# Feed-forward products of a two-layer transformer kernel as pairs of 64-row tiles

## The chip, the cores and the metric

One core of a Trainium2 chip. The metric is device time in microseconds (us). Five engines run side by side, each through its own queue in order: TensorE (PE; its weight loads are listed apart as PEld), VectorE (DVE), ScalarE (ACT), GpSimd (POOL) and SyncE (SP), which issues the DMAs. PE accumulates into PSUM, eight banks of 128 partitions by 512 float32; the other operands lie in SBUF, 128 partitions wide.

## The reference

Two identical layers over 2048 tokens of width 448: multi-query attention (16 heads of 28, one shared key and value head), then a SwiGLU feed-forward with 1792 hidden columns. Each half normalises its input and adds its result to the residual.

```python
def _B_ref(x, w_gate, w_up, w_down):
    g = _silu(x @ w_gate)
    u = x @ w_up
    return (g * u) @ w_down

x = A_x
x = x + _A_ref(_layernorm(x, axis=-1), A_wq, A_wk, A_wv, A_wo)
x = x + _B_ref(_layernorm(x, axis=-1), B_w_gate, B_w_up, B_w_down)
x = x + _A_ref(_layernorm(x, axis=-1), A_wq, A_wk, A_wv, A_wo)
x = x + _B_ref(_layernorm(x, axis=-1), B_w_gate, B_w_up, B_w_down)
```

## The kernel before

All products but those of values and transposes use a shortened float32 (`F32R`). To keep the precision, each operand is split into a high and a low part, and a product is the sum of high by high, high by low and low by high.

The feed-forward is cut into **units**: one unit is one slice of 128 hidden columns (`fc`, 14 of them) for one block of 512 tokens (`c`, 4 of them). The slices run in groups of two (`groups`), and within a group the order is block by block, for each block both slices (`n` = 0, 1): 8 units a group, 7 groups, 56 units a layer, 112 in all. The width of 448 is four chunks: three of 128 rows and one of 64. The last chunk is stacked: the token tile `xh[:, 3]` holds the high part in rows 0 to 63 and the low part in rows 64 to 127, and the weights' chunk is loaded twice, one copy below the other.

`unit` (L683) does this. On PE, `product_T` (L258) gives gate's product into one PSUM bank with 11 matmuls of 128 rows (three for each of the three full chunks, two for the stacked one), then up's product into a second bank with 11 more. ACT takes the silu of gate's bank (L695), DVE multiplies it by up's bank (L696), ACT rounds the result to the high part of h (L697), and DVE takes the low part (L698). `flush` (L679) then issues what an earlier unit left in `pend`: its `down` (L635), 12 matmuls, for each of four token tiles three into one of the four banks `HIGH`; and behind a block's second slice `accumulate` (L643), four adds of these banks to the residual `xres` on DVE (L647). So the down products of a unit stand on PE behind the products of the next one. The banks `LOW` serve gate and up by turns, two units deep.

The token tiles come from `turned` (L673): 16 transposes on PE (`flip`, L242), copies of the high part on ACT, low parts on DVE, and then `norm` (L236) of the block after, whose statistics, scaling and shifting run on DVE with a step on POOL between. In the first group this stands in the second unit (n = 1) of blocks 1 and 2, ahead of `flush`; `rest` (L716) calls it once more ahead of the first of its units, for block 1. The first two units of a layer (block 0) are issued inside the attention, ahead of `rest`.

In the last group of layer 0, `accumulate` also issues the statistics and scaling of the next layer's first normalisation, and two blocks are turned and projected to queries at once. `weights` (L156) loads and splits a slice of weights (DMA, then POOL) three slices ahead. `stack` (L306) brings the queries of one of 16 steps of the attention from DRAM into one of three tiles `qts`.

All engines run in the order in which the code issues the work (`manual_schedule`, L82); what waits for what is found from the tiles that are read and written.

Of the kernel before, what the change touches and what calls it, by code (L numbers as in the profile page):

```python
# [8 lines left out]
F32 = mybir.dt.float32  # L9
# [6 lines left out]
P = 128  # L16
S = 2048
D = 448
# [44 lines left out]
def forward(  # L63
# [67 lines left out]
    def dma(dst, src):  # L131
        nc.sync.dma_start(dst.bitcast(F32), src.bitcast(F32))  # L132
# [69 lines left out]
            part(z, load(z))  # L202
        return [], (wh, wl)

    def xtile(pool):
        return (
            pool.tile([P, 4, 512], F32R, name="xh"),
            pool.tile([P, 3, 512], F32R, name="xl"),
        )

    def norm_steps(c, pool=pers):
# [29 lines left out]

    def flip(got, tiles, ks=range(4), place=None):  # L242

        xh, xl = tiles
        for k in ks:
            pt = place if place is not None else bank(LOW)[1]
            for t in range(4):
                nc.tensor.transpose(pt[:, P * t : P * t + P], got["x"][:, t, P * k : P * k + P], ident)  # L248
            if place is not None:
                nc.vector.tensor_copy(xh[:, k, :], pt)  # L250
            else:
                nc.scalar.copy(xh[:, k, :], pt)
            if k < 3:
                nc.vector.tensor_tensor(xl[:, k, :], pt, xh[:, k, :], ALU.subtract)
            else:
                nc.vector.tensor_tensor(xh[64:128, k, :], pt[64:128, :], xh[64:128, k, :], ALU.subtract)

    def product_T(po, a_h, a_l, tiles, tick=None):  # L258

        xh, xl = tiles  # L260
        seq = []
        for k in range(3):
            seq += [(a_h[k], xh[:, k, :]), (a_h[k], xl[:, k, :]), (a_l[k], xh[:, k, :])]
        seq += [(a_h[3], xh[:, 3, :]), (a_l[3], xh[:, 3, :])]
        for i, (a, b) in enumerate(seq):
            nc.tensor.matmul(po, a, b, start=(i == 0), stop=(i == len(seq) - 1))  # L266
            if tick:
                tick()

    GR = [(c, g) for c in range(NC) for g in range(NG)]  # L270

    class Attention:
# [129 lines left out]
        def project(self):  # L402

            c, m = self.order[self.seen]
            for f in self.plan.get((self.seen, 0), ()):
                f()
            for o in self.order[self.seen : self.seen + 2]:
                if o[1] == 3:
                    self.turned(o[0])
            load = self.waiting.pop(0) if self.waiting else None  # L410
            self.q(c, m)
            if load:
                load()
            for f in self.plan.get((self.seen, 1), ()):
                f()
            self.seen += 1
            if c == 0 and m < 3:
                if not full and m < 2:
# [63 lines left out]
        def scores(self, ff):  # L482
            next(switch)
            with tc.tile_pool(name=f"at{self.layer}", bufs=1) as wp:
# [104 lines left out]
                ff.norms[1] = got1  # L589
                for i in range(len(GR)):  # L590
                    for k2 in range(NT // 2):
                        if k2 == 2 and 2 < i + 2 < len(GR):
                            self.stack(i + 2)
                        if k2 == 5 and i + 2 < len(GR) and not full:
                            self.high(i + 2)
                        if i in (2, 3) and k2 == 4:
                            load_wo(i - 2)
                        if k2 == 4 and 10 < i <= 11 + FG:
                            ff.W[i - 11] = weights(i - 11)

                        free = cycle(i, k2)
                        if k2 == 5 and i + 1 < len(GR) and full:
                            self.places[i + 1](free[:, 0, :])
                        if i == 6 and 0 < k2 < 5:
                            flip(got, X0, [k2 - 1], free[:, 0, :])
                        while late:
                            pv(*late.pop(0))
                        late += [(i, 2 * k2), (i, 2 * k2 + 1)]
                        if 8 * i + k2 in due:
                            due.pop(8 * i + k2)()  # L610
                        if i in (5, 9) and k2 > 2:
                            for f in (fs if i == 5 else fs1)[2 * k2 - 6 : 2 * k2 - 4]:
                                f()
# [15 lines left out]
    class FeedForward:  # L629
        def __init__(self, layer):  # L630
            self.layer, self.X, self.W, self.norms = layer, {}, {}, {}
            self.pend, self.soon, self.dn = [], [], {}
            self.nxt = Attention(1) if layer == 0 else None

        def down(self, fs, fc, d, hh, hl):  # L635
            _, _, dh, dl = self.W[fc]
            for t in range(4):
                ts_ = slice(P * t, P * t + P)
                po = d[t][:, 0:D]
                for z, (a, b) in enumerate(((hh, dh), (hh, dl), (hl, dh))):  # L640
                    nc.tensor.matmul(po, a[:, ts_], b, start=(fc == fs[0] and z == 0), stop=(fc == fs[-1] and z == 2))  # L641

        def accumulate(self, gi, c, d):  # L643
            end = gi == len(groups) - 1
            for t in range(4):
                r = xres[:, 4 * c + t, :]
                nc.vector.tensor_tensor(r, d[t][:, 0:D], r, ALU.add)  # L647
# [24 lines left out]

        def turned(self, c):  # L673
            self.X[c] = xtile(self.xbp)
# [8 lines left out]
        def unit(self, gi, c, n):  # L683
            fs = groups[gi]
            fc = fs[n]
            h, l, _, _ = self.W[fc]
            pg = []
            for b in range(2):
                po = bank(LOW)[1]
                product_T(po, [h[:, k, b, :] for k in range(4)], [l[:, k, b, :] for k in range(4)], self.X[c])  # L690
                pg.append(po)
# [3 lines left out]
            nc.scalar.activation(sg, pg[0], AF.Silu)  # L695
            nc.vector.tensor_tensor(sg, pg[1], sg, ALU.mult)  # L696
            nc.scalar.copy(hh, sg)  # L697
            nc.vector.tensor_tensor(hl, sg, hh, ALU.subtract)  # L698
# [11 lines left out]
            self.pend.append(lambda: self.down(fs, fc, d, hh, hl))  # L710
            if n == len(fs) - 1:
                self.pend.append(lambda: self.accumulate(gi, c, d))
            if c == NC - 1 and fc + FG + 1 < NF:
                self.pend.append(lambda: self.W.__setitem__(fc + FG + 1, weights(fc + FG + 1)))

        def rest(self, xb):  # L716
            self.xbp = xb.enter_context(tc.tile_pool(name=f"xb{self.layer + 1}", bufs=3))
            self.turned(1)
            for gi, fs in enumerate(groups):
                for c in range(NC):  # L720
# [5 lines left out]
            if self.nxt:  # L726
                self.nxt.open()
                self.nxt.project()
            self.flush()

    for t in range(4):
        nc.sync.dma_start(xres[:, t, :], xs[:, t, :])
# [68 lines left out]
```

## Time and profile before

| | |
|---|---|
| median of 3 runs | 2103.12 us (2102.9 to 2103.98) |
| profiled execution | 2104.14 us, its span from the first to the last instruction 2102.1 us |
| mean granted TensorE clock | 0.993 |
| attention of layer 0, value products | until 622.8 us |
| feed-forward of layer 0 | 622.9 to about 1083 us, with layer 1's first query products among it |
| feed-forward of layer 1 | 1663.4 us to the end |

Times in the rows below are from the span's start. A row of the chain in order of time gives start, length, engine, tile, line and count. A row of the timeline gives start, length, engine, line, operation, output and inputs with their shapes, the count, and in brackets how long the engine was idle before and what ended that. A group's row gives busy time and mean duration in ns. The matrices' durations overlap, as they are pipelined: the distance between two starts is what one costs. In a matmul's row, "128*128" are rows and columns of the tile of the array, "128x512" what streams through.

### The profile page before, as it was taken

The page shows a single profiled execution, that of the slowest core. Times are in us where ns is not written, and L with a number is a line of the kernel's source. Part 1 is how long each engine was busy: PE and PEld are TensorE (multiplying, and loading weights), DVE is VectorE, ACT ScalarE, POOL GpSimd, SP SyncE. Part 2 cuts the span into 40 slices and gives each one's busy share as a digit, 9 for nine tenths or more (in the row PEclk, how much of TensorE's full clock was granted, in tenths as well). Part 3 has the DMA queues.
Part 4 walks back from the last instruction along what each step waited for, and adds up shares of the span by engine and source line. Part 5 has one row for each costly group of instructions (what it writes and reads, how often), then busy time and mean ns, then how long its engine had stood idle before and what let it go on. Part 6 is the DMA issues. An engine that isn't in the chain of part 4 may idle for free.

```text
span 2102.1 us, 28049 instructions
## 1 busy us (share of the span) xinstructions
PE 2054.0 (98%) x11073; PEld 1371.4 (65%) x11073; DVE 573.8 (27%) x1150; ACT 1181.1 (56%) x1600; POOL 365.5 (17%) x386
## 2 busy tenths in 40 slices
PE   7899999999999999999989999999999999999998
PEld 5544544545458888888775445455454588888887
DVE  6110131211105333333551112212111163333333
ACT  2599799798982111111127997988979621111111
POOL 5202010103201111111231111011212111111100
PEclk9999999999999999999999999999999999999999
DMA  6413122122200111110142222121322000111001
GB/s 183 137 30 70 30 54 49 35 53 60 49 6 20 29 29 29 29 29 10 32 130 79 55 51 50 29 56 29 70 43 48 25 10 21 29 29 30 29 1 72
DMA packets 98540, 97.21 MB, mean 46 GB/s; under 512 B 28992, under 2 KB 68320, under 8 KB 98400
## 3 DMA queue, kind: packets, MB, share of 16 engines
q1 hardware_dynamic: 98400, 95.34, 18.3%
q8 instruction: 89, 1.46, 0.3%
q14 instruction: 51, 0.42, 0.1%
HBM read 73.53 MB, written 18.61 MB: 44 GB/s over the span
## 4 chain that ended last, share of the span: by engine, by line
PE 91%; DMA 3%; DVE 2%; SPq 2%; POOL 1%; ACT 1%; issue 0%; ACTq 0%; POOLq 0%; DVEq 0%
PE bank L266 27%; PE bank L546 22%; PE pair L511 16%; PE bank L641 12%; PE bank L511 7%; PE pair L503 3%; DMA qd<-q 1%; PE pair L338 1%; PE bank L503 1%; DMA o<-rd 1%; PE bank L248 1%; DVE stats L217 1%; DVE xres L647 0%; SPq L132 0%; SPq L456 0%
## 5 line engine op out<-in xcount | busy, mean ns | idle before, releaser
L518 ACT ACTIVATE pt<-pair 128x1024 f32<-128x1024 f32 x768 | 763.5, 1029 | 0.7 <-PE pair L511 0.7
L546 PE MATMUL bank<-pt,vsb 128*32 128x512 f32 x4096 | 492.1, 598 | 0.0
L511 PE MATMUL pair<-qstack,kstack 128*128 128x512 f32 x1536 | 399.7, 395 | 1.2 <-ACT q L442 1.2
L518 ACT ACTIVATE pt<-bank 128x512 f32<-128x512 f32 x512 | 308.2, 602 | 90.8 <-PE bank L511 84.2
L266 PE MATMUL bank<-xh,wgh 128*128 128x512 f32 x896 | 349.1, 390 | 0.3
L266 PE MATMUL bank<-xh,wgl 128*128 128x512 f32 x896 | 348.5, 389 | 0.0
L511 PEld LDWEIGHTS pair<-qstack,kstack 128*128 128x128 f32 x1536 | 286.4, 188 | 62.3 <-ACT q L442 2.1
L695 ACT ACTIVATE sg<-bank 128x512 f32<-128x512 f32 x112 | 67.2, 600 | 372.4 <-PE bank L266 358.6
L641 PE MATMUL bank<-wdh,h 128*128 128x448 f32 x896 | 273.0, 365 | 0.0
L546 PEld LDWEIGHTS bank<-pt,vsb 128*32 128x32 f32 x4096 | 107.2, 109 | 245.0 <-issue 243.9
L266 PE MATMUL bank<-xl,wgh 128*128 128x512 f32 x672 | 261.5, 389 | 0.0
L697 ACT CAST h<-sg 128x512 fp32r<-128x512 f32 x112 | 69.5, 620 | 319.9 <-DVE sg L696 319.9
L511 PE MATMUL bank<-qstack,kstack 128*128 128x512 f32 x512 | 218.8, 427 | 2.7 <-ACT pt L518 2.7
L511 PEld LDWEIGHTS bank<-qstack,kstack 128*128 128x128 f32 x512 | 96.0, 187 | 156.1 <-ACT pt L518 144.4
L579 POOL TENSOR_TENSOR o<-o 128x512 f32<-128x512 f32 x32 | 41.2, 1287 | 898.7 <-DMA o<-rd 712.3
L266 PEld LDWEIGHTS bank<-xh,wgl 128*128 128x128 f32 x896 | 168.2, 188 | 35.0
L266 PEld LDWEIGHTS bank<-xh,wgh 128*128 128x128 f32 x896 | 168.2, 188 | 34.8 <-issue 1.7
L696 DVE TENSOR_TENSOR sg<-bank,sg 128x512 f32<-128x512 f32 x112 | 77.5, 692 | 414.9 <-PE bank L266 398.8
L641 PEld LDWEIGHTS bank<-wdh,h 128*128 128x128 f32 x896 | 168.1, 188 | 14.8
L641 PE MATMUL bank<-wdl,h 128*128 128x448 f32 x448 | 162.5, 363 | 0.0
L558 DVE COPY o<-bank 128x512 f32<-128x512 f32 x32 | 22.1, 692 | 456.1 <-PE bank L546 456.1
L266 PEld LDWEIGHTS bank<-xl,wgh 128*128 128x128 f32 x672 | 126.1, 188 | 23.5
(98 smaller groups left out, 1507.7 us busy)
## 6 DMA issues: line engine op xcount, KB each, us to landing
qstack<-qd SPq DMA_DIRECT2D x128, 224.0 KB
qd<-q SPq DMA_DIRECT2D x24, 512.0 KB
o<-rd SPq DMA_DIRECT2D x32, 256.0 KB
qhigh<-qd SPq DMA_DIRECT2D x128, 56.0 KB
wdr<-in_B_w_down_dram SPq DMA_DIRECT2D x28, 224.0 KB
wr<-in_B_w_gate_dram SPq DMA_DIRECT2D x28, 192.0 KB
wr<-in_B_w_up_dram SPq DMA_DIRECT2D x28, 192.0 KB
out_dram<-xres SPq DMA_DIRECT2D x16, 224.0 KB
```

The source lines that it names most:

```text
L217: nc.vector.bn_stats(stats[:, 4 * c + t, :], xres[:, 4 * c + t, :])
L266: nc.tensor.matmul(po, a, b, start=(i == 0), stop=(i == len(seq) - 1))
L503: nc.tensor.matmul(po[:, 0:D], a[:, g, ts_], b[:, g, :], start=(g + z == 0), stop=(g == NG - 1 and z == 2))
L511: nc.tensor.matmul(sp[:, e, :], kt_[:, P * kt : P * kt + P], qts[i % 3][:, j, :], start=True, stop=True)
L518: nc.scalar.activation(pt[:, 0 : len(which), :], sp[:, 0 : len(which), :], AF.Exp, scale=SCALE)
L546: nc.tensor.matmul(accs[i][32 * j : 32 * j + 32, :], vsb[:, kt, :], pts.pop((i, (kt, j))), start=(kt == 0), stop=(kt == NT - 1), skip_grou ...
L558: nc.vector.tensor_copy(oraw, accs.pop(i))
L579: nc.gpsimd.tensor_tensor(rb, oraw, rb, ALU.mult)
L641: nc.tensor.matmul(po, a[:, ts_], b, start=(fc == fs[0] and z == 0), stop=(fc == fs[-1] and z == 2))
L695: nc.scalar.activation(sg, pg[0], AF.Silu)
L696: nc.vector.tensor_tensor(sg, pg[1], sg, ALU.mult)
L697: nc.scalar.copy(hh, sg)
```

## The change

Each of gate's and up's products becomes two lists of 64-row matmuls, one for the lower rows (0 to 63) and one for the upper (64 to 127) of every chunk (`by_rows`). A list has ten or eleven: three for each full chunk, one for the last, and one more for the low part of the last chunk's weights, which gate takes in the lower rows and up in the upper; the product of both low parts is left out. `side_by_side` issues two lists by turns: first gate's lower with up's upper rows (11 pairs), then up's lower with gate's upper (10 pairs). Since both halves of a product go to the same bank, `between` has DVE read one column of each of the two banks after the first half, and the second half waits for these reads. Between the halves stands the first of two steps of the earlier unit's `down`; `down` gives two steps of six pairs (for each of two pairs of token tiles three), in the second the rows are swapped, and `between` stands behind the first step. The second step comes with `flush`, behind the silu and what follows it.

`accumulate` now adds token tiles 0 and 2 on DVE; tiles 1 and 3 are copied by ACT and added by POOL. `turned` stands in the first unit of a block (n = 0), behind `flush`. Up's upper rows need the high part of the last chunk in rows 64 to 127; it is kept in `qts[2]`, which attention doesn't use then. Therefore the queries for attention's third step (i = 2) are loaded during its first, for both layers, and `qts[2]` is set to zero at the end of layer 0's feed-forward. The first two units of each layer still use `product_T`.

```diff
+    def by_rows(upper, n, w, tiles):
+
+        h, l = w[:2]
+        xh, xl, xd = tiles
+        rs = slice(64, 128) if upper else slice(0, 64)
+        seq = []
+        for k in range(3):
+            seq += [(h[rs, k, n, :], xh[rs, k, :]), (h[rs, k, n, :], xl[rs, k, :]), (l[rs, k, n, :], xh[rs, k, :])]
+        seq.append((h[rs, 3, n, :], xh[rs, 3, :]))
+        if n == upper:
+            seq.append((l[rs, 3, n, :], xd[rs, :] if upper else xh[rs, 3, :]))
+        return seq
+
+    def side_by_side(lower, upper):
+
+        assert len(lower) == len(upper)
+        for two in zip(lower, upper):
+            for po, (a, b), start, stop in two:
+                nc.tensor.matmul(po, a, b, start=start, stop=stop, skip_group_check=True)
+
+    seen = pers.tile([P, 4], F32, name="seen")
+
+    def between(*pos):
+
+        for i, po in enumerate(pos):
+            nc.vector.tensor_copy(seen[:, i : i + 1], po[:, 0:1])
...
-                        if k2 == 2 and 2 < i + 2 < len(GR):
+                        if k2 == 2 and i + 2 < len(GR):
...
         def down(self, fs, fc, d, hh, hl):
+
+
             _, _, dh, dl = self.W[fc]
-            for t in range(4):
-                ts_ = slice(P * t, P * t + P)
-                po = d[t][:, 0:D]
-                for z, (a, b) in enumerate(((hh, dh), (hh, dl), (hl, dh))):
-                    nc.tensor.matmul(po, a[:, ts_], b, start=(fc == fs[0] and z == 0), stop=(fc == fs[-1] and z == 2))
+            self.flip = 1 - self.flip
+            one, two = ((0, 1), (2, 3)) if self.flip else ((2, 3), (0, 1))
+
+            def step(ts, first):
+                lists = []
+                for upper, half in enumerate(ts):
+                    rs = slice(64 * upper, 64 * upper + 64)
...
+                side_by_side(*lists)
+                if first:
+                    between(*d)
+
+            return [lambda: step((one, two), True), lambda: step((two, one), False)]
 
         def accumulate(self, gi, c, d):
             end = gi == len(groups) - 1
-            for t in range(4):
+            for t in (0, 2, 1, 3):
                 r = xres[:, 4 * c + t, :]
-                nc.vector.tensor_tensor(r, d[t][:, 0:D], r, ALU.add)
+                if t % 2 == 0:
+                    nc.vector.tensor_tensor(r, d[t][:, 0:D], r, ALU.add)
+                else:
+                    s = self.stage.tile([P, D], F32, name="stage")
+                    nc.scalar.copy(s, d[t][:, 0:D])
+                    nc.gpsimd.tensor_tensor(r, s, r, ALU.add)
...
+            pg = [bank(LOW)[1] for _ in range(2)]
+            if self.X[c][2] is not None:
+                lists = [by_rows(upper, b, w, self.X[c]) for b in range(2) for upper in range(2)]
+                ends = [(i == 0, False) for i in range(11)], [(False, i == 9) for i in range(10)]
+                side_by_side(
+                    [(pg[0], o, *e) for o, e in zip(lists[0], ends[0])],
+                    [(pg[1], o, *e) for o, e in zip(lists[3], ends[0])],
+                )
+                between(*pg)
+                self.pend.pop(0)()
+                side_by_side(
+                    [(pg[1], o, *e) for o, e in zip(lists[2], ends[1])],
+                    [(pg[0], o, *e) for o, e in zip(lists[1], ends[1])],
+                )
+            else:
+                for b in range(2):
+                    product_T(pg[b], *([v[:, k, b, :] for k in range(4)] for v in w[:2]), self.X[c])
...
-            if gi == 0 and n == len(fs) - 1 and 0 < c < NC - 1:
+            self.flush()
+            if gi == 0 and n == 0 and 0 < c < NC - 1:
                 self.turned(c + 1)
-            self.flush()
```

Three places show what this makes of the order. The first is PE in the first unit of block 1 in layer 0, from the end of the first half; `wgh` and `wgl` are the weights' high and low parts, `wdh` and `wdl` those of the down weights, `qstack_97` the tile that holds the last chunk's high part. Before, behind up's last matmul of that unit:

```order
L266 MATMUL bank_4965<-xh,wgh 128x512
L266 MATMUL bank_4965<-xh,wgl 128x512
L641 MATMUL bank_4968<-wdh,h_5032 128x448
L641 MATMUL bank_4968<-wdl,h_5032 128x448
L641 MATMUL bank_4968<-wdh,h_5032 128x448
L641 MATMUL bank_4969<-wdh,h_5032 128x448
```

Now, the last pairs of the first half and the first of the down step:

```order
L295 MATMUL bank_4965<-xh,wgh 128x512
L295 MATMUL bank_4966<-xh,wgh 128x512
L295 MATMUL bank_4965<-xh,wgl 128x512
L295 MATMUL bank_4966<-qstack_97,wgl 128x512
L295 MATMUL bank_76<-wdh,h_5033 128x448
L295 MATMUL bank_4969<-wdh,h_5033 128x448
L295 MATMUL bank_76<-wdl,h_5033 128x448
L295 MATMUL bank_4969<-wdl,h_5033 128x448
```

And six rows further on, the end of the down step and the start of the second half:

```order
L295 MATMUL bank_77<-wdh,h_5033 128x448
L295 MATMUL bank_4970<-wdh,h_5033 128x448
L295 MATMUL bank_4966<-xh,wgh 128x512
L295 MATMUL bank_4965<-xh,wgh 128x512
L295 MATMUL bank_4966<-xl,wgh 128x512
L295 MATMUL bank_4965<-xl,wgh 128x512
```

Neighbours go to different banks by turns, and six pairs of the earlier unit's down products stand between the halves. The second place is DVE in two units of the steady part (`sg` is the silu, `h` the low part of h, `seen` the reads of `between`). Before, behind one block's accumulation:

```order
L647 TENSOR_TENSOR xres<-bank_77,xres 128x448
L696 TENSOR_TENSOR sg<-bank_4967,sg 128x512
L698 TENSOR_TENSOR h_5458<-sg,h_5458 128x512
L696 TENSOR_TENSOR sg<-bank_4965,sg 128x512
L698 TENSOR_TENSOR h_5513<-sg,h_5513 128x512
L647 TENSOR_TENSOR xres<-bank_4968,xres 128x448
```

Now:

```order
L768 TENSOR_TENSOR sg<-bank_4966,sg 128x512
L770 TENSOR_TENSOR h_5994<-sg,h_5994 128x512
L703 TENSOR_TENSOR xres<-bank_4969,xres 128x448
L703 TENSOR_TENSOR xres<-bank_76,xres 128x448
L302 COPY seen<-bank_4967 128x1
L302 COPY seen<-bank_4968 128x1
L302 COPY seen<-bank_4969 128x1
L302 COPY seen<-bank_4970 128x1
L302 COPY seen<-bank_76 128x1
L302 COPY seen<-bank_77 128x1
L768 TENSOR_TENSOR sg<-bank_4968,sg 128x512
```

Two adds are gone from DVE, and six reads stand ahead of each multiplication; the first two of them, which the second half waits for, come behind the adds. The third place is DVE in the opening, where block 2 has been turned and block 3 is normalised (`stats`, `mv` and `xn` are the statistics and the normalised tokens). Before:

```order
L218 BN_AGGR mv<-stats 128x2
L230 TENSOR_SCALAR xn<-xres,mv,rstd 128x448 x4
L696 TENSOR_TENSOR sg<-bank_4965,sg 128x512
L698 TENSOR_TENSOR h_5304<-sg,h_5304 128x512
L647 TENSOR_TENSOR xres<-bank_4968,xres 128x448
```

Now:

```order
L220 BN_AGGR mv<-stats 128x2
L232 TENSOR_SCALAR xn<-xres,mv,rstd 128x448 x4
L302 COPY seen<-bank_4967 128x1
L302 COPY seen<-bank_4968 128x1
L302 COPY seen<-bank_4969 128x1
L302 COPY seen<-bank_4970 128x1
L302 COPY seen<-bank_76 128x1
L302 COPY seen<-bank_77 128x1
L768 TENSOR_TENSOR sg<-bank_4968,sg 128x512
```

Behind the normalisation stood the next multiplication; now the reads stand there.

More of the change, by code (lines that the diff above doesn't have):

```diff
@@ L203, in load_wqkv, with xtile @@
         return [], (wh, wl)
-    def xtile(pool):
+    def xtile(pool, again=None):
         return (
@@ L208, in xtile @@
             pool.tile([P, 3, 512], F32R, name="xl"),
+            again,
         )
@@ L242, in flip @@
     def flip(got, tiles, ks=range(4), place=None):
-        xh, xl = tiles
+        xh, xl, xd = tiles
         for k in ks:
@@ L248, in flip @@
                 nc.tensor.transpose(pt[:, P * t : P * t + P], got["x"][:, t, P * k : P * k + P], ident)
-            if place is not None:
-                nc.vector.tensor_copy(xh[:, k, :], pt)
-            else:
[L252 to L256, printed above, removed]
+            copy = nc.vector.tensor_copy if place is not None else nc.scalar.copy
+            if k < 3:
+                copy(xh[:, k, :], pt)
+                nc.vector.tensor_tensor(xl[:, k, :], pt, xh[:, k, :], ALU.subtract)
+                continue
+            if xd is None:
+                copy(xh[:, k, :], pt)
+                high = xh[64:128, k, :]
+            else:
+                copy(xh[0:64, k, :], pt[0:64, :])
+                copy(xd[64:128, :], pt[64:128, :])
+                high = xd[64:128, :]
+            nc.vector.tensor_tensor(xh[64:128, k, :], pt[64:128, :], high, ALU.subtract)
     def product_T(po, a_h, a_l, tiles, tick=None):
-        xh, xl = tiles
+        xh, xl = tiles[:2]
         seq = []
@@ L416, in project @@
             self.seen += 1
-            if c == 0 and m < 3:
-                if not full and m < 2:
+            if c == 0 and m < 2:
+                if not full:
                     self.waiting.append(lambda: self.high(m))
@@ L685, in unit @@
             fc = fs[n]
[L686 to L691, printed above, removed]
+            w = self.W[fc]
+            pg = [bank(LOW)[1] for _ in range(2)]
[5 more added lines that the diff above has]
+                    [(pg[1], o, *e) for o, e in zip(lists[3], ends[0])],
+                )
+                between(*pg)
[3 more added lines that the diff above has]
+                    [(pg[0], o, *e) for o, e in zip(lists[1], ends[1])],
+                )
+            else:
+                for b in range(2):
+                    product_T(pg[b], *([v[:, k, b, :] for k in range(4)] for v in w[:2]), self.X[c])
             two = halves("h2")
@@ L709, in unit @@
             d = self.dn[c]
-            self.pend.append(lambda: self.down(fs, fc, d, hh, hl))
+            self.pend += self.down(fs, fc, d, hh, hl)
             if n == len(fs) - 1:
@@ L717, in rest @@
             self.xbp = xb.enter_context(tc.tile_pool(name=f"xb{self.layer + 1}", bufs=3))
+            self.stage = xb.enter_context(tc.tile_pool(name=f"stage{self.layer}", bufs=2))
+            dma(qts[2][64:128, 0, :], self.X[0][0][0:64, 3, :])
+            self.X[0] = (*self.X[0][:2], qts[2][:, 0, :])
             self.turned(1)
@@ L729, in rest @@
             self.flush()
+            if self.nxt:
+                nc.gpsimd.memset(qts[2].bitcast(F32), 0.0)
     for t in range(4):
```

15 lines of the change are left out of this document (13 added, 2 removed).

## The prediction, made before the changed kernel ran

> **What bounds the kernel now.** First the page: busy shares, then the chain of work that ended last, by engine and by line.
>
> ```profile
> PE 2054.0 (98%) x11073; PEld 1371.4 (65%) x11073; DVE 573.8 (27%) x1150; ACT 1181.1 (56%) x1600; POOL 365.5 (17%) x386
> ...
> PE 91%; DMA 3%; DVE 2%; SPq 2%; POOL 1%; ACT 1%; issue 0%; ACTq 0%; POOLq 0%; DVEq 0%
> ```
>
> TensorE is the chain; the others matter only where PE waits for them. Next that chain in order of time: start, length, what. The first two rows are the steady feed-forward, the rest its opening in layer 0.
>
> ```profile
> 843.72 4.99 PE bank L266 x22
> 851.13 4.99 PE bank L266 x22
> ...
> 646.39 0.70 DVE xl L254
> ...
> 647.13 5.28 PE bank L266 x22
> 652.41 2.43 PE bank L641 x12
> 654.84 4.99 PE bank L266 x22
> 659.83 1.75 PE bank L248 x16
> 661.58 2.42 PE bank L641 x12
> 664.00 5.01 PE bank L266 x22
> ```
>
> A unit (128 hidden columns by 512 tokens) takes 851.13 - 843.72 = 7.41 us: 22 products in 4.99, so 0.2267 each, and 12 downs in 2.42, so 0.2017 each. There is no wait in it. How much of 0.2267 is the stream of 512 columns itself? Late in layer 0 the clock is halved for a while after waits:
>
> ```profile
> 1103.90 1.09 PE L248 MATMUL bank<-ident,xn 128*128 128x128 f32 x4 [5.25 <-ACT q L442]
> ...
> 1106.05 0.63 PE L266 MATMUL bank<-xh,wl 128*128 128x512 f32 x1
> 1106.47 0.63 PE L266 MATMUL bank<-xh,wh 128*128 128x512 f32 x1
> 1106.90 0.63 PE L266 MATMUL bank<-xl,wh 128*128 128x512 f32 x1
> ...
> 1105.60:1109.40 3.80, 3.80 (x10) 2.97 (x9) 1.26 (x2) 0.12 (x1) 0.24 (x1) 0.50 0.47 152
> ```
>
> The last row is a table by stretch; its 0.50 is the granted clock. Starts lie (1106.90 - 1106.05)/2 = 0.425 to 0.427 apart, so at the full clock the stream needs 0.2135, and 0.1868 for 448 columns. The rest, 0.013 and 0.015, is a gap at every change of weights.
>
> **The products in pairs.** The gate's and up's 22 matmuls of 128 rows become 21 pairs of 64 rows, since the term of both low parts in the last chunk goes; the 12 downs become 12 pairs. If two tiles run beside one another, call the time of a pair X (512 columns) and Y (448). No 64-row tile is in the trace. Bounds: the bare stream, X = 0.2135 and Y = 0.1868; and each tile paying its gap after the other, X = 0.240, Y = 0.2166. The nearest row with tiles is the value product of attention, 32 columns a tile, with the forms' group behind it:
>
> ```profile
> 615.31 1.92 PE L546 MATMUL bank<-pt,vsb 128*32 128x512 f32 x16
> ...
> L546 PE MATMUL bank<-pt,vsb 128*32 128x512 f32 x4096 | 492.1, 598 | 0.0
> ```
>
> Sixteen of 0.598 us fit into 1.92, so column tiles do overlap, about (1.92 - 0.60)/3 = 0.44 for four. I take the gap once per pair, as in a full-array matmul: **X = 0.2267, Y = 0.2017**. That is 21 x 0.2267 + 12 x 0.2017 = 7.18 a unit, 0.23 less than before, if nothing waits.
>
> The Trainium skill, "TensorE: Matmul & The Clock Gate", Part 3, states that tiles start about 4 ns apart and that a pack lasts one matmul plus 4 ns per further tile, yet reports 3.07 times, not 4, for four row tiles. By the 4 ns the 50 couples counted below would come out 10 us later than in my sum (couple 14.63 + 0.26); 3.07 speaks for the dearer bound. No run here shows either yet.
>
> **The wait behind the accumulation.** Gate and up now end together, at the end of the second half, so the silu no longer lies under up's product. The durations, from the timeline:
>
> ```profile
> 704.97 0.39 PE L266 MATMUL bank<-xh,wgl 128*128 128x512 f32 x1
> 705.40 0.60 ACT L695 ACTIVATE sg<-bank 128x512 f32<-128x512 f32 x1 [3.51 <-PE bank L266]
> ...
> 700.55 0.69 DVE L696 TENSOR_TENSOR sg<-bank,sg 128x512 f32<-128x512 f32 x1 [5.34 <-PE bank L266]
> 701.27 0.62 ACT L697 CAST h<-sg 128x512 fp32r<-128x512 f32 x1 [2.69 <-DVE sg L696]
> 701.92 0.69 DVE L698 TENSOR_TENSOR h<-sg,h 128x512 fp32r<-128x512 f32 x1 [0.69 <-ACT h L697]
> 702.53 2.21 DVE L647 TENSOR_TENSOR xres<-bank,xres 128x448 f32<-128x448 f32 x4
> ```
>
> (704.97 is the last matmul of that gate's product.) Let T be the end of a unit's products on PE. The silu starts 0.43 after the last matmul's start, that is T+0.21; the multiplication at T+0.84; the high part at T+1.57; the low part at T+2.22; the first add 0.61 later, at T+2.83; the second at T+3.36 (the four start 0.53 apart), done at T+3.97. With 0.06 for the wake-up, PE may write the first two banks again at T+4.03. PE gets there after six down pairs and eleven product pairs: T + 1.21 + 2.49 = T+3.70. So every second unit, the one behind an accumulation, has a **wait of 0.33 us** (0.56 at the bare stream, 0.09 at the dear bound). Without an accumulation nothing waits: the high part is there at T+2.2, the low one at T+2.9. The small reads between the halves have six down pairs (1.2 us) or ten product pairs (2.3) over them; they cost about this each, up to four in a row, which fits:
>
> ```profile
> L567 DVE TENSOR_SCALAR under<-rs 128x16 f32<-128x16 f32 x64 | 11.2, 175 | 111.1 <-DMA rs<-o 110.0
> L141 POOL TENSOR_TENSOR wdl<-wdr,wdh 128x448 fp32r<-128x448 f32 x28 | 32.3, 1153 | 2.3
> ```
>
> The two adds moved to ACT and POOL (the second row prices one) are done long before their rows are read again: nothing.
>
> A couple of units, before: 14.82. After: 42 x 0.2267 + 24 x 0.2017 + 0.33 = 14.69, so -0.13. Some 25 couples per layer are steady, 50 in all: **-6.5 us**.
>
> **The openings.** Where tokens are normalised and turned during the first group, the order shows the statistics, the scaling and only then the small reads on DVE, and PE's second half waits for these. Before, the multiplication stood there, which PE needed much later. One such block:
>
> ```profile
> 649.03 0.63 DVE L217 BATCH_NORM_STATS2 stats<-xres 128x6 f32<-128x448 f32 x1
> ...
> 653.47 1.78 DVE L230 TENSOR_SCALAR xn<-xres,mv,rstd 128x448 f32<-128x448 f32 x4 [1.41 <-POOL rstd L223]
> 655.28 0.69 DVE L696 TENSOR_TENSOR sg<-bank,sg 128x512 f32<-128x512 f32 x1
> ```
>
> It holds DVE for 655.28 - 649.03 = 6.25 us. First unit: PE starts at 647.13 as before, is through half a product and a down step at 650.84, and waits until 655.28 + 2 x 0.175 = 655.6: 4.8 us. Its products end at 657.87 (T), the down step at 659.08, the transposes (1.75) at 660.83, the next half and down step at 664.53. DVE has its adds done at T+3.97 = 661.84, then the split of the turned block, as before 649.03 - 646.39 = 2.64, then 6.25, then the reads: 671.1. PE waits 6.6 us, and is through that unit at 671.1 + 2.27 + 1.21 = 674.6, where the kernel before stood at 664.00: 10.6 us late, **+21.2 us** for two layers. The third turned block has no statistics behind it: nothing. Before, these blocks lay under 7.4 us of PE work; that cover is gone.
>
> **Smaller terms.** The first down of a layer runs its two steps back to back, with the tail of one matmul and four small reads bare, 0.9: +1.8. In the last group of layer 0 the statistics of three blocks stand before the reads in the same way, 3.97 + 6.25 + 0.35 against PE's 4.91, so up to 5.7 each; but the kernel before waits there too:
>
> ```profile
> 1021.48 2.80 PE L248 MATMUL bank<-ident,xn 128*128 128x128 f32 x16
> ...
> 1025.22 0.50 PE L266 MATMUL bank<-xh,wh 128*128 128x512 f32 x1 [0.94 <-DVE xl L254]
> ```
>
> That is (2.80 - 1.75) + 0.94 = 2.0 for one, and later waits for DMAs may absorb more: between 0 and 17 in all, I take +5. At the very end the down steps wait for both parts of h (1.0), for the reads (0.9), and for the copy and add on ACT and POOL in place of DVE's (1.6): +3.5. After waits of 5.25 us the clock above was halved for ten matmuls, 10 x 0.21 = 2.1; two waits of 6.6: +4.2 (0 to 10). One DMA of queries that moves into the first attention group is wanted two groups later: nothing.
>
> **The sum**, against the profiled execution's 2104.1 (the median of the runs is 1 lower): -6.5 + 21.2 + 1.8 + 5 + 3.5 + 4.2 = +29, so **2133 us**.
>
> **Rivals.** *The gap closes.* Two tiles that change weights in turn may leave none: X = 0.2135, Y = 0.1868. Couple: 13.45 + 0.56 = 14.01, -0.81 x 50 = -40.5; openings 20.6, the rest 14.5: -5.4, 2099; with last group and clock at nothing 2089, with no wait behind the accumulation too 2070. It decides from X of about 0.2155 down. For it: column tiles overlap; against: those rows are another form of matmul. *The gap is paid twice*, X = 0.240, Y = 0.2166: couple 15.28 + 0.09, +27.5, and with 21.8 + 14.5 it is +64, 2168. *The weight loads bind*: 16 transposes, a load of 128 columns each, took 1.75 us, 0.109 each; two in turn are 0.219, under 0.2267 but over 0.2017. Then Y = 0.219, couple 14.78 + 0.22, +9, in all +45, 2149. *The tiles don't run beside one another*, the change not doing what it says: 84 x 0.2267 + 48 x 0.2017 = 28.7 a couple, +13.9 x 54 = +751, 2855.
>
> **How the numbers follow.** Gap once, 0.37: 2133. Gap closed, 0.32, of which 0.24 end faster: 2070 to 2103. Gap twice or loads, 0.26: 2149 to 2168. In turn, 0.05: 2855. 0.2% is about what a measurement of this kernel can tell from no change. Faster 0.27 (with a little for what I overlook), same 0.12, slower 0.61. The range leaves out the last case, the lowest of the closed gap and a little above the doubled one: 2078 to 2170.
>
> **What would show it.** Pair spacing in the steady units (0.2135, 0.2267 or 0.240) and of the downs; a wait of 0.3 to 0.6 at every second unit, released by DVE's add of the residual; PE waits of 4.8 and 6.6 us in each opening, released by the reads into `seen`; halved clock behind them. No waits there, or pairs far off 0.21 to 0.24, would make it wrong.

## The result and the profile after

The changed kernel takes 2158.64 us (median of 4 runs, 2156.98 to 2160.23) beside 2103.01 us for the kernel before on the same chip: a ratio of 1.0264, 95% interval 1.0247 to 1.0282. It is slower, as forecast, and inside the range, but by 55.6 us where the sum said 29. The profiled execution's span went from 2102.1 to 2155.1 us.

The page after, busy shares and then the chain that ended last, by engine:

```profile
PE 2079.6 (96%) x14577; PEld 1420.3 (66%) x14577; DVE 584.1 (27%) x1702; ACT 1233.1 (57%) x1718; POOL 495.8 (23%) x499
...
PE 88%; DVE 5%; DMA 3%; SPq 2%; ACT 1%; POOL 1%; issue 1%; ACTq 0%; POOLq 0%; DVEq 0%
```

TensorE's share of the chain fell from 91% to 88% and DVE's rose from 2% to 5%: TensorE now stands behind VectorE at some places. Where they are is read from the list of what PE waited for, over the whole span (total us, times, longest):

```profile
PE bank L295 <- DVE seen L302: 28.8, 9, 4.8
PE bank L295 <- DVE xl L254: 5.6, 4, 1.4
```

Both rows are new: before, no unit of the feed-forward's openings waited for either. The first is the forecast wait for the small reads; the second, for the low part of a turned token block, was not forecast.

In the steady feed-forward the chain in order of time is unbroken, as before, and its pieces are couples of units:

```profile
839.13 14.87 PE bank L295 x127
...
854.00 14.87 PE bank L295 x127
```

A couple of units takes 14.87 us; it took 14.82, and 14.69 was forecast.

Now the two stretches with waits in layer 0, the first seven units (from the start of the first silu to the start of the eighth) and the last seven. A row gives from and to, length, then busy time and count for PE, PEld, DVE, ACT and POOL, then the granted clock and the DMA share. First the kernel before:

```profile
625.65:690.57 64.92, 64.78 (x323) 56.56 (x322) 36.85 (x70) 14.49 (x26) 11.98 (x17) 1.00 0.06 17
994.52:1064.22 69.70, 66.27 (x304) 55.81 (x303) 34.88 (x67) 14.39 (x26) 14.71 (x18) 0.98 0.13 37
```

The same in the changed kernel, and some short stretches behind single waits:

```profile
621.36:709.16 87.80, 77.36 (x542) 65.10 (x541) 37.40 (x105) 18.73 (x35) 18.20 (x23) 0.92 0.06 14
1013.71:1103.72 90.01, 71.65 (x531) 58.91 (x529) 42.72 (x111) 17.66 (x34) 26.49 (x32) 0.89 0.10 27
653.20:656.00 2.80, 2.80 (x14) 2.24 (x16) 0.30 (x4) 0.00 (x0) 0.00 (x0) 0.50 0.00 0
663.10:666.30 3.20, 3.20 (x18) 2.55 (x16) 3.06 (x8) 0.00 (x0) 0.00 (x0) 0.50 0.02 5
687.00:690.20 3.20, 3.20 (x18) 3.01 (x16) 0.63 (x1) 0.00 (x0) 0.00 (x0) 0.50 0.00 0
1010.00:1036.00 26.00, 23.70 (x208) 21.20 (x206) 12.90 (x32) 5.39 (x10) 11.69 (x8) 1.00 0.11 29
1041.50:1045.00 3.50, 3.50 (x16) 2.81 (x18) 0.35 (x4) 0.00 (x0) 0.09 (x1) 0.50 0.00 0
...
800.00:816.00 16.00, 16.00 (x145) 14.51 (x144) 5.93 (x19) 3.69 (x7) 2.33 (x2) 1.00 0.00 1
```

The opening grew by 22.9 us. Of these 3.5 are no loss, since the silu that ends the stretch now stands behind ten more pairs (2.3) and a down step (1.2); so the opening of layer 0 costs 19.4. In the first row PE is idle for 87.80 - 77.36 = 10.4 us, where it was idle for 0.1, and the mean clock is 0.92 instead of 1.00, which is worth about 0.08 x 87.8 = 7.0. The last group grew by 20.3 in the same way: idle 18.4 instead of 3.4, clock 0.89 instead of 0.98. In steady state (last row) the clock is full.

| part | forecast, us | measured, us | how it was measured |
|---|---|---|---|
| steady couples | -6.5 | +1.6 | some 44.5 of them: 304.55 instead of 303.95 from silu to silu between those stretches in layer 0, the same in layer 1, and 0.4 in layer 1's last group |
| openings, with first down steps and their halved clock | +27.2 | +38.8 | 2 x 19.4 |
| last group of layer 0 | +5 | +20.3 | the rows above |
| end of each layer's feed-forward | +3.5 | +3.0 | from the last silu on, with the 3.5 put back and without the queries |
| queries loaded earlier | 0 | -10.3 | value products start 5.15 earlier in layer 0, and 5.13 sooner behind the last down step in layer 1 |
| sum | +29 | +53.4 | spans: +53.0; the other 0.4 lies in the attention |

### The profile page after: what moved, and what is told of

It reads as the page before. It is cut to its first block, busy times and chain, and to the rows that moved or that the text cites. A ratio compares the mean times of both kernels' runs of the same rounds, so it can differ in the third digit from the quotient of the medians.

```text
span 2155.1 us, 36057 instructions
## 1 busy us (share of the span) xinstructions
PE 2079.6 (96%) x14577; PEld 1420.3 (66%) x14577; DVE 584.1 (27%) x1702; ACT 1233.1 (57%) x1718; POOL 495.8 (23%) x499
## 4 chain that ended last, share of the span: by engine, by line
PE 88%; DVE 5%; DMA 3%; SPq 2%; ACT 1%; POOL 1%; issue 1%; ACTq 0%; POOLq 0%; DVEq 0%
PE bank L295 36%; PE bank L580 21%; PE pair L545 16%; PE bank L545 7%; PE bank L273 3%; PE pair L537 3%; PE pair L372 1%; DVE stats L219 1%; DMA qstack<-qd 1%; PE bank L537 1%; DVE xn L232 1%; DVE h L770 1%; DVE xres L703 0%; DVE sg L768 0%; DMA o<-rd 0%
## 5 line engine op out<-in xcount | busy, mean ns | idle before, releaser
L295 PE MATMUL bank<-xh,wgh 64*128 64x512 f32 x1728 | 500.3, 398 | 33.2 <-DVE seen L302 26.7
L295 PE MATMUL bank<-xh,wgl 64*128 64x512 f32 x1404 | 402.6, 395 | 0.0
L295 PE MATMUL bank<-xl,wgh 64*128 64x512 f32 x1296 | 374.0, 397 | 0.0
L295 PE MATMUL bank<-wdh,h 64*128 64x448 f32 x1792 | 364.9, 368 | 6.6 <-DVE xres L703 2.6
L295 PEld LDWEIGHTS bank<-xh,wgh 64*128 64x128 f32 x1728 | 303.7, 189 | 55.0 <-DVE seen L302 29.3
L295 PEld LDWEIGHTS bank<-wdh,h 64*128 64x128 f32 x1792 | 270.7, 185 | 43.1 <-DVE xres L703 14.3
L295 PEld LDWEIGHTS bank<-xh,wgl 64*128 64x128 f32 x1404 | 249.0, 190 | 13.0
L295 PE MATMUL bank<-wdl,h 64*128 64x448 f32 x896 | 245.9, 366 | 0.0
L295 PEld LDWEIGHTS bank<-xl,wgh 64*128 64x128 f32 x1296 | 228.3, 190 | 11.6
L295 PEld LDWEIGHTS bank<-wdl,h 64*128 64x128 f32 x896 | 151.2, 185 | 4.1
```

The source lines that it names most:

```text
L295: nc.tensor.matmul(po, a, b, start=start, stop=stop, skip_group_check=True)
```

## The experiments

The first four ran on one chip (the kernel before: 2101.88 us), the last three on another (2101.47), and the result's kernel before took 2103.01; so a difference between times of different groups is good to about 1.5 us.

### The queries' loads alone

The kernel before, with only the earlier load of the third step's queries.

```diff
-            if c == 0 and m < 3:
-                if not full and m < 2:
+            if c == 0 and m < 2:
+                if not full:
...
-                        if k2 == 2 and 2 < i + 2 < len(GR):
+                        if k2 == 2 and i + 2 < len(GR):
```

> The kernel before, with one part of the change alone: the queries of attention's third step are loaded during its first step, in both layers, and not in the stretch that leads up to the attention. In the changed kernel the value products of layer 0 start 5.15 us earlier than before, and the stretch from the last down product of layer 0 to the value products of layer 1 is 5.1 us shorter. Theory: both come from this part, so about 2103 - 10 = 2093 us. Rival: the prelude is shorter for another reason (other buffers, another order of the queue), then 2103 us, within 2.

Measured: 2091.58 us, ratio 0.9949 (0.9932 to 0.9966). The DMA that the prediction priced at "nothing" is worth 10.3 us, and it is a gain. The chain in order of time shows where, in the stretch before the first value products. Before:

```profile
51.63 6.99 DMA qd<-q
...
60.01 4.74 DMA qd<-q
...
68.80 4.73 DMA qd<-q
...
87.00 1.85 PE bank L546 x16
```

And with the edit:

```profile
54.48 4.29 DMA qd<-q
...
60.72 14.27 PE bank L266 x55
...
81.26 1.85 PE bank L546 x16
```

The chain into attention went through one store of queries after another, each behind SP's queue. Without the third step's loads in that queue, it goes through 55 products on PE for 14 us, and the value products start 5.7 us earlier. Over the whole span, PE's waits ahead of its transposes for ACT's copies of the queries fell from 15.2 to 6.1 us. The load is indeed wanted much later; what counted was what stood behind it in the queue.

### The reads of the banks on ACT

The changed kernel, with the small reads on ACT, so that they no longer stand behind the norm on DVE.

```diff
-            nc.vector.tensor_copy(seen[:, i : i + 1], po[:, 0:1])
+            nc.scalar.copy(seen[:, i : i + 1], po[:, 0:1])
```

> The changed kernel with the small reads between the halves on ACT in place of DVE. Theory: the openings (20 us a layer) and the last group of layer 0 (some 15 to 20 us) are dear because the reads stand behind the normalisation on DVE, and the halved clock follows from those waits: the waits of 4.3 and 2.6 us in each opening and the three of 5.15 us in the last group go or shrink to what the turned tokens need, and the halved clock goes with them; about 2158 - 40 = 2118 us, between 2105 and 2130. Waits of 1.66 us ahead of the first half behind each turned block, released by DVE's low parts, stay. Rival: the loss lies in the pairs and the banks, and the reads only show it: 2150 us or more.

Measured: 2116.79 us, ratio 1.0072 (1.0055 to 1.0089), so 41.9 us of the loss are back. The same two stretches as above:

```profile
619.09:695.21 76.12, 72.03 (x541) 62.64 (x541) 33.00 (x65) 23.59 (x75) 18.20 (x23) 0.98 0.06 16
998.84:1071.90 73.06, 68.01 (x530) 56.99 (x528) 34.97 (x65) 22.68 (x76) 24.63 (x28) 0.98 0.12 34
```

The opening falls by 11.7 us, the last group by 17.0, and the clock returns to 0.98 in both. Idle time fell by 6.3 and 13.3 us, so the rest, 5.4 and 3.6, is mostly the clock. With layer 1's opening (9.9, from silu to silu) that makes 38.5 of the 41.9. What is left in the opening is the wait for the turned block:

```profile
PE bank L295 <- DVE xl L254: 3.4, 2, 2.1
```

### The adds ahead of the low part

The changed kernel, with DVE's two adds ahead of the low part of h, in all groups but the last. The rival was that the low part would then be stretched by POOL's adds running beside it.

```diff
-            nc.vector.tensor_tensor(hl, sg, hh, ALU.subtract)
+            last = gi == len(groups) - 1
+            if last:
+                nc.vector.tensor_tensor(hl, sg, hh, ALU.subtract)
             self.flush()
+            if not last:
+                nc.vector.tensor_tensor(hl, sg, hh, ALU.subtract)
```

> The changed kernel with DVE's two adds of the residual ahead of the low part of h, in all groups but the last. Theory: the steady wait at every second unit (0.48 us) ends when the second add is done, at T+4.2; ahead of the low part it is done 0.6 us sooner, so the wait goes, and 50 couples gain 0.48 each: 2158 - 24 = 2134 us. Rival: the low part, now beside POOL's adds (1.18 us each, two in a row), is held until these end, as it was stretched to 2.46 us beside POOL's 2.39 us split in the kernel before; then it is done at about T+5.6 in place of T+3.1, the down products' third pair waits for it, and the time is 2158 us or some 20 to 40 us more.

Measured: 2129.89 us, ratio 1.0134 (1.0117 to 1.0151). The timeline of DVE and POOL shows the new order, and the chain in order of time what it does to PE, 80 us and 701 matmuls in one piece:

```profile
914.05 1.14 DVE L703 TENSOR_TENSOR xres<-bank,xres 128x448 f32<-128x448 f32 x2
...
915.12 0.68 DVE L775 TENSOR_TENSOR h<-sg,h 128x512 fp32r<-128x512 f32 x1
915.30 2.61 POOL L707 TENSOR_TENSOR xres<-stage,xres 128x448 f32<-128x448 f32 x2 [11.77 <-ACT stage L706]
```

```profile
879.85 80.15 PE bank L295 x701
```

Each unit now takes 7.19 us, where they took 7.19 and 7.67 by turns: the 0.48 is the wait of PE for the banks that DVE's adds free, and some 40 couples of it (the last groups keep the old order) are 19 us of the 27.6 by which the span fell. Most of the rest came in the openings, 3.1 each. Layer 0's, in the table by stretch:

```profile
619.55:704.21 84.66, 74.04 (x542) 62.43 (x542) 37.56 (x105) 18.73 (x36) 18.31 (x23) 0.96 0.06 15
```

PE is idle for 84.66 - 74.04 = 10.6 us there, as much as in the changed kernel (10.4), but the mean clock is 0.96 instead of 0.92. The waits for the turned block are 0.9 and 1.1 us here, not 1.4, and no halved clock follows them: two halved stretches an opening instead of four, so these 3.1 us are the clock's. The rival falls: the low part takes 0.68 us beside POOL's adds, and in all 96 units with the new order between 0.679 and 0.694.

### The two lists one behind the other

The changed kernel with the same matmuls, but each row group's list as a whole, the lower one first.

```diff
-        for two in zip(lower, upper):
-            for po, (a, b), start, stop in two:
+        for one in (lower, upper):
+            for po, (a, b), start, stop in one:
```

> The changed kernel with the two lists of every pair one behind the other: all of the lower rows' matmuls first, then all of the upper rows'. Theory: a 64-row matmul takes as long as one of 128 rows (0.2267 us) and the pairs cost 0.2267 because two tiles overlap; without turns a couple of units takes 84 x 0.2267 + 48 x 0.2017 = 28.7 us in place of 14.9, and the kernel about 2158 + 13.9 x 54 = 2909 us. Rival: 64-row matmuls take half the time each, one after the other, and nothing overlaps: 2158 us, spacing 0.113 us.

Measured: 2336.85 us, a single run, so without an interval. Neither theory holds: a unit takes 9.12 us, where 7.19 would be full overlap and 42 x 0.2267 + 24 x 0.2017 = 14.4 none. PE's timeline, around the end of a list of products:

```profile
901.44 0.39 PE L295 MATMUL bank<-xh,wgh 64*128 64x512 f32 x1
901.67 0.39 PE L295 MATMUL bank<-xl,wgh 64*128 64x512 f32 x1
901.68 0.47 PE L295 MATMUL bank<-wdh,h 64*128 64x448 f32 x1
901.90 0.39 PE L295 MATMUL bank<-xh,wgl 64*128 64x512 f32 x1
901.99 0.36 PE L295 MATMUL bank<-wdl,h 64*128 64x448 f32 x1
902.13 0.39 PE L295 MATMUL bank<-xh,wgh 64*128 64x512 f32 x1
902.19 0.36 PE L295 MATMUL bank<-wdh,h 64*128 64x448 f32 x1
902.36 0.39 PE L295 MATMUL bank<-qstack,wgl 64*128 64x512 f32 x1
```

A list keeps its distance of 0.23 a matmul, so one row group alone is no faster than a pair. The downs are issued behind all of these products, yet the first of them starts at 901.68, ahead of three products that were issued before it: the other row group was free. So issuing by turns is what fills the array, and some overlap comes without it. The Trainium skill, "TensorE: Matmul & The Clock Gate", Part 3, says that matmuls start and end strictly in order; by the starts of this trace they don't where the row groups differ.

### Both mends together

Reads on ACT and adds ahead, the two edits above.

> The changed kernel with both repairs: reads between the halves on ACT, and DVE's two adds ahead of the low part of h in all groups but the last. Theory: the two act on different waits, so their gains add up: the reads gave 2158.6 - 2116.8 = 41.8, the adds 2158.6 - 2129.9 = 28.7, together 2088 us, a unit at 7.19 us throughout. That is below the kernel before (2102) and below it with late queries (2091.6). Rival: both end at the same chain of DVE, so the second brings less: 2100 us or more.

Measured: 2092.42 us, ratio 0.9956 (0.994 to 0.9973). The two alone brought 41.9 and 28.7, together 66.2 of 70.6: nearly independent, and with them the change is a gain. It is no more of one than the queries' loads alone (2091.58).

### And the turned block in the second unit

The kernel of the experiment above, with the next block turned in a block's second unit, ahead of `flush`, as it was before the change; the low part is issued ahead of it there.

```diff
-            if last:
+            if last or n:
                 nc.vector.tensor_tensor(hl, sg, hh, ALU.subtract)
+            if gi == 0 and n == len(fs) - 1 and 0 < c < NC - 1:
+                self.turned(c + 1)
             self.flush()
-            if not last:
+            if not (last or n):
                 nc.vector.tensor_tensor(hl, sg, hh, ALU.subtract)
-            if gi == 0 and n == 0 and 0 < c < NC - 1:
-                self.turned(c + 1)
```

> As the one before, and the turned blocks back in the second unit (n = 1), ahead of the down step, as in the kernel before. Theory: in the first unit the transposed tiles' banks are held until DVE has done the multiplication, the adds and two low parts (waits of 2.4 and 1.6 us ahead of the next products, with halved clock behind the first); in the second unit no adds stand between and the normalisation has a whole unit more, so some 4 to 6 us a layer go: 2088 - 10 = 2078 us. Rival: the place makes no difference, as the banks are held by the low parts wherever they stand: 2088 us.

Measured: 2085.47 us, ratio 0.9924 (0.9908 to 0.9941), the fastest of all. The opening of layer 0 in the table by stretch:

```profile
620.23:691.75 71.52, 70.67 (x541) 60.17 (x541) 32.71 (x65) 23.56 (x75) 18.38 (x23) 1.00 0.07 17
```

PE is idle for 0.9 us and the clock is full throughout. Less the 3.5, the opening is 3.1 longer than before, instead of 19.4. It was expected at 2078, that is 10 below an expected 2088; from the 2092.42 of the experiment above it brought 7.0, and the openings still hold some of the rest.

This kernel and the first experiment share the queries' gain. They differ by 6.1 us, so that is what the products in pairs, with all that came along with them, were worth at best here: the steady stretches are 9.0 us shorter in each layer (294.93 instead of 303.95), and openings and ends take most of it back; the intervals of the two ratios overlap, so a gain is likely and not certain.

### All adds on DVE

The changed kernel, with the four adds back on DVE, to double the wait behind the accumulation. The rival was that the wait has nothing to do with the adds.

```diff
-                if t % 2 == 0:
+                if True:
                     nc.vector.tensor_tensor(r, d[t][:, 0:D], r, ALU.add)
```

> The changed kernel with all four adds of the residual on DVE, as before, in the order 0, 2, 1, 3. Theory: the wait at every second unit is set by the adds' end; the two further adds (0.53 us each) end at about T+5.3, the fourth pair of the down step, which writes the third and fourth bank, is reached at T+4.9, and the reads for the second half come behind them: 0.4 to 0.6 us more per couple of units, 2158.6 + 52 x 0.5 = 2185 us. Rival: the first two adds alone decide, so moving the others to ACT and POOL brought nothing: 2158 us.

Measured: 2219.60 us, ratio 1.0565 (1.0548 to 1.0583), 35 more than expected. The sign and the size per couple hold: about half of the couples are 8.13 + 7.19, 0.46 longer. But nearly every group also has units of 9 to 11 us. One of them, in the timeline of POOL, DVE and ACT:

```profile
912.44 0.60 ACT L767 ACTIVATE sg<-bank 128x512 f32<-128x512 f32 x1 [5.21 <-PE bank L295]
...
914.31 1.15 POOL L141 TENSOR_TENSOR wdl<-wdr,wdh 128x448 fp32r<-128x448 f32 x1
914.45 1.56 DVE L770 TENSOR_TENSOR h<-sg,h 128x512 fp32r<-128x512 f32 x1 [0.69 <-ACT h L769]
...
921.41 0.60 ACT L767 ACTIVATE sg<-bank 128x512 f32<-128x512 f32 x1 [6.99 <-PE bank L295]
```

From silu to silu it is 8.97 us: the low part of h took 1.56 instead of 0.69, beside POOL's split of a weight, and all adds stand behind it. In the changed kernel the low part is stretched too, to some 1.57 us twelve times (at 711.18, for one, beside a split that POOL began at 711.05), but in units with no adds behind it, and these keep their 7.20 us. That POOL's adds stand there in the same queue as the splits, and so move them to such units, is one explanation; it was not tried by itself.

## Why the prediction was right in direction and short in size

**The products in pairs: right.** "I take the gap once per pair" was 0.2267 and 0.2017. Steady units, PE's timeline with the ends of the two lists and the engines behind them:

```profile
804.24 0.59 PE L295 MATMUL bank<-xh,wgh 64*128 64x512 f32 x2
...
804.92 0.59 PE L295 MATMUL bank<-xh,wgh 64*128 64x512 f32 x2
805.15 0.57 PE L295 MATMUL bank<-wdh,h 64*128 64x448 f32 x2
...
805.60 0.60 ACT L767 ACTIVATE sg<-bank 128x512 f32<-128x512 f32 x1 [5.22 <-PE bank L295]
...
806.36 0.39 PE L295 MATMUL bank<-xh,wgh 64*128 64x512 f32 x1
...
808.22 1.15 DVE L703 TENSOR_TENSOR xres<-bank,xres 128x448 f32<-128x448 f32 x2
...
808.63 0.39 PE L295 MATMUL bank<-xh,wgl 64*128 64x512 f32 x1
808.83 0.39 PE L295 MATMUL bank<-qstack,wgl 64*128 64x512 f32 x1
808.98 0.91 PE L295 MATMUL bank<-wdh,h 64*128 64x448 f32 x2
...
809.42 0.18 PEld L295 LDWEIGHTS bank<-wdh,h 64*128 64x128 f32 x1 [0.28 <-DVE xres L703]
...
813.25 0.60 ACT L767 ACTIVATE sg<-bank 128x512 f32<-128x512 f32 x1 [4.80 <-PE bank L295]
```

The four pairs of products from 804.24 to 805.15 are 0.2275 each to the row's last digit, the six pairs of downs from 805.15 to 806.36 are 0.2017, and a unit without a wait is 7.19 where 7.18 was worked out. The rivals that closed the gap or paid it twice needed 0.2135 or 0.240 for a pair of products, and the one bound on weight loads 0.219 for a pair of downs; none of these is there. By the 4 ns for a further tile that the Trainium skill states ("TensorE: Matmul & The Clock Gate", Part 3), a unit would come to an estimated 7.18 + 33 x 0.004 = 7.31; the trace's 7.19 does not agree.

**The wait behind the accumulation: the mechanism right, 0.48 instead of 0.33.** The step that failed is "The silu starts 0.43 after the last matmul's start, that is T+0.21". T is 805.15 here, and the silu starts at 805.60, T+0.45: the lists don't run in step. A pair's row lasts 0.59 where a single matmul's lasts 0.39, so the second tile starts 0.20 behind the first. At the end of the next half the last matmul of one list starts at 808.63 and that of the other at 808.83, so a product ends up to 0.2 later than its pair count says. All on DVE moves with it, and the second add ends at 808.22 + 1.15 = 809.37, T+4.22 instead of T+3.97. The weight load behind it, at 809.42, is released by that add, as forecast, and from silu to silu the unit takes 813.25 - 805.60 = 7.65. With the adds ahead of the low part the wait is gone (7.19 flat). So the couple's gain was -0.13 on paper and +0.03 on the chip (304.55 - 303.95 over 20.5 couples).

**The openings: the waits right in sum, the clock behind them mis-sized.** PE's timeline in layer 0, the rows with a wait ahead:

```profile
653.13 0.80 PE L295 MATMUL bank<-xh,wgh 64*128 64x512 f32 x2 [3.95 <-DVE seen L302]
...
661.60 1.09 PE L295 MATMUL bank<-xh,wgh 64*128 64x512 f32 x2 [1.38 <-DVE xl L254]
...
670.02 0.80 PE L295 MATMUL bank<-xh,wgh 64*128 64x512 f32 x2 [2.23 <-DVE seen L302]
...
1041.47 0.80 PE L295 MATMUL bank<-xh,wgh 64*128 64x512 f32 x2 [4.80 <-DVE seen L302]
```

"PE waits until ... 4.8" is 3.95 here, and "PE waits 6.6 us" is 2.23, because PE came there late: between the two stands a wait of 1.38 for the turned block's low part, whose banks are wanted by the next products and whose DVE work now stands behind that unit's multiplication, low part and adds. That wait comes again in the third block (another 1.4 by the list of waits), of which the prediction said "The third turned block has no statistics behind it: nothing". Together with 1.06 behind the first down steps this makes 10.0 of the 10.4 us of idle time per layer, against 12.3 forecast.

The forecast's clock term was "two waits of 6.6: +4.2", one halved stretch a layer. The trace shows four per opening at 0.50, each 3.4 us long by its record of the clock, behind the waits of 1.4 (the rows of 663.10 and 687.00) as well as behind the longer ones. Some 0.6 of these 13.7 us fall in the waits themselves, so they cost (13.7 - 0.6)/2 = 6.5 us a layer. Some 2.5 us of an opening's 19.4 are not split further. The mean clock of the whole span fell from 0.993 to 0.986, which is 2155.1 x 0.014 - 2102.1 x 0.007 = 15.5 us of full-speed time, not 4.2; that is an upper bound of what it cost, since part of it lies in waits. So the number of halved stretches was the error, four for one. The row of the price was also read short: in the kernel before, the clock is at 0.50 from the end of the wait of 5.25 at 1103.90 to about 1109.8, so the half clock behind that wait cost 2.9 and not the 2.1 of ten matmuls.

**The last group of layer 0: a term mis-sized, +20.3 for +5.** "Later waits for DMAs may absorb more: between 0 and 17 in all, I take +5." Nothing was absorbed: three waits of 4.8, within the price ("up to 5.7 each"), and behind each of them the halved clock for some 3.8 us more (0.50 in the row of 1041.50 above), which the bound of 17 left out. With the reads on ACT 17.0 us of it go.

**The queries: mis-sized, -10.3 for nothing.** The step asked when the data is wanted, not what stood behind its loads in SP's queue. **The end** came out at +2.3 at the very end, for which +3.5 was forecast, and +0.7 at the end of layer 0, which was not priced.

By terms, the misses are +8.1 (couples), +11.6 (openings), +15.3 (last group), -10.3 (queries) and -0.5, together +24.2. That the time stayed well inside the range is in part luck: without the queries' gain it would be about 2169, at the range's end of 2170. One figure of the rivals was also summed wrongly: 2070, for the closed gap with no wait behind the accumulation, still holds the last group and the clock; with these at nothing too the terms give 2061.

The halved clock was never taken away wholly by itself; the adds ahead come closest, with equal idle time, two halved stretches fewer and 3.1 us less in each opening. What makes up the 0.013 us that a pair costs beyond its stream stays open as well.

## What to carry to other kernels

When a product is split so that two halves write the same bank, look up what stands on the synchronising engine's queue ahead of the read between them, at the openings and ends of stages first: more than the whole loss came from 21 of the 112 units. Price a wait of TensorE of 2 us or more as itself plus the half clock behind it, which cost 1.5 to 2.9 us here; for waits of 1 to 1.6 us reckon with it or without, since both came out here. And price a moved load by its place in the queue of transfers, not by when its data is used. A change that loses time may still be worth having in another order: here three small moves turned +2.6% into -0.8%, and most of that 0.8% is the queries' gain.

## What the runs showed of the hardware that was not expected

Matmuls on different row groups of the array overtake one another by up to three places (starts at 901.68 beside 901.90, 902.13 and 902.36), and two lists that are issued by turns run 0.2 us apart. A list on half of the rows is no faster alone (0.23 a matmul) than beside another list. The clock fell to 0.50 for 3.4 us behind waits of only 1.4 us in the openings, while a wait of 1.60 (PE started again at 1018.94, in the row of 1010.00), one of 1.06 (at 631.28) and the steady waits of 0.48 left it at 1.00; so the length of a wait alone did not decide it, and what did was not tried. DVE's subtraction of two operands in SBUF took 1.56 us instead of 0.69 beside POOL's split of a weight, and 0.68 where POOL's adds started behind it.
